# Attention and MLP gradients of one decode step: batch 1's middle paced differently, its kept heads moved in the second pass, and the MLP output in a stream of its own

## The chip, the cores and the metric

The kernel runs on one core of one Trainium2 chip. The metric is the device time of a launch in microseconds (us), the median of five runs. A profiled execution gives a span (first to last instruction) and a trace of every instruction and transfer.

## The reference

One decode step of a pre-norm transformer block, forward and backward: two sequences (B = 2), width D = 640, 32 heads of 128, a cache of 4096 keys and values for each head, an MLP of 1728 with ReLU.

```python
def _fwd_reference(A_x, A_k_cache, A_v_cache, A_wq, A_wo, B_x, B_w1, B_w2):
    ...
    h = x + _A_ref(_layernorm(x, axis=-1), A_k_cache, A_v_cache, A_wq, A_wo)
    h2 = h + _B_ref(_layernorm(h, axis=-1), B_w1, B_w2)
    return h2

def reference(A_x, A_k_cache, A_v_cache, A_wq, A_wo, B_w1, B_w2, B_x, grad_out):
    ...
    _out, _vjp = jax.vjp(_f, A_x, A_k_cache, A_v_cache, A_wq, A_wo, B_w1, B_w2)
    _grads = _vjp(grad_out)
```

`_A_ref` is softmax attention of one query against the cache, followed by `wo`. The eight outputs are the forward result (out_0) and the gradients of x (out_1), the K cache (out_2), the V cache (out_3), wq (out_4), wo (out_5), w1 (out_6) and w2 (out_7). The cache gradients are the bulk: 64 pairs of sequence and head, each with 1 MiB of K gradient and 1 MiB of V gradient in bf16.

## The kernel before

The work goes over the 64 pairs of batch and head twice.

*Pass one* (`p1_iter`, i = 0 to 65) loads K and V of a pair, transposes K on TensorE, computes scores, softmax, the attention output and a 128 x 128 matrix MT for each head. At its end for a batch, `middle_gen(b)` does what lies between forward and backward: output projection, layer norm, MLP forward, MLP backward, layer norm backward, and then, for groups of heads (`go_group`), the gradient of each head's output. The dot products with the rows of w1 (15 of them) and wo (32, one for each head) are VectorE instructions (L649, in `ttr`). `ln_fwd` and `ln_bwd` are chains of short VectorE instructions with small TensorE column sums between them.

*Pass two* (`p2_iter`, j = 0 to 64, called a turn here) takes one pair: it loads V again as W (L457, on SP's queue), transposes it as float32 pairs (L436), copies the result out of PSUM on ScalarE (L441), multiplies it with the head's output gradient (L449), forms the row of score gradients (gsp, L835), and makes the outer products gK and gV on VectorE (L822, two halves each). POOL's queue stores them (L860 and L879). The first turns run inside pass one; from i = 41 on every second iteration carries one, so that turns 0 to 12 lie there and turns 13 to 64 follow alone. `turns` gives the order: for each batch first the "kept" heads, whose V tile of pass one is kept in SBUF and not loaded again (six of batch 0, the last five, 27 to 31, of batch 1), then the others. Batch 1's kept heads stand at places 32 to 36.

Turn j of batch 1 needs its head's `go_group`. If that isn't done when the turn begins, `bg_until` runs the background to that mark at once.

The program is written out in one order for each engine by an interleaver. A turn has seven steps k = 0 to 6. After each step three background streams may go on: `bg` (the middle), `bg2` (`fin_gen`: the weight gradients out_7, out_6, out_5, out_4, as matmuls L926 into a PSUM bank and copies L935 and L933 into an "ot" tile, stored by ScalarE's queue) and `bg3` (`gx_gen`: the gradient of x through wq, as transposes L993, copies L995 and matmuls L1003). A stream earns credit at a rate in each step and spends it as its generator yields: 0.5 for a plain yield, or the number that it yields. `RATES` is for the middle, `RATE2` and `RATE3` for the others. `slot` says in which steps the middle may issue a dot product. `wait(n)` lets n x `spread` steps pass between a producer and its consumer.

`mlp_out` (out_0 = h + MLP forward) loads w2 in three parts and multiplies it (L709). Before, it is the end of batch 1's `middle_gen`, in stream `bg`.

The large tiles live in 12 "homes" of 1 MiB, and a thirteenth after w1's tile is released. Each belongs to a tag: `ld` (loads), `g` (gK, gV), `f` (output tiles), `q` (w2 and wq parts of the two streams). `share` sets how many each tag is to have; a home changes its tag when it is next given back. At turn 13 it is 8 for `ld` and 4 for `g`, of which the kept tiles hold 5; once the kept heads of batch 1 are through it is 4, 4, 3 and 2:

```python
        elif fin is not None and j >= H + KEPT[1] - 1:
            share(ld=4, g=4, f=3, q=2)
```

`fin_gen` and `gx_gen` begin at the turn after w1's dot products are done; `gx_gen` waits for every `go_group`.

Of the kernel before, what the change touches and what calls it, by code (L numbers as in the profile page):

```python
# [9 lines left out]
ALU = mybir.AluOpType  # L10
# [5 lines left out]
def kernel(  # L16
# [20 lines left out]
    nc = tc.nc  # L37

    B, Sq, D = A_x.shape
    _, H, Sk, Dh = A_k_cache.shape  # L40
# [17 lines left out]
    def f_kc(c):  # L58
        return 128 if c < NFF else F_rem
# [45 lines left out]
    def give(t, to=None):  # L105
        tag, k, _ = home_of.pop(id(t))
        to = to or goes_to(tag)
        owned[tag] -= 1
        owned[to] += 1
        free[to] += 1  # L110
        homes[to].append(k)
        given_at[k] = step[0]
# [25 lines left out]
    spread = [1]  # L138
# [253 lines left out]
    NP1 = len(pairs)  # L392
    KEPT = (6, 5)
    turns = [(b, h) for b in range(B) for h in (*range(H - KEPT[b], H), *range(H - KEPT[b]))]
    turn_of = {bh: j for j, bh in enumerate(turns)}
    kept = {(b, h) for b in range(B) for h in range(H - KEPT[b], H)}
    u_bank = [None]
# [254 lines left out]
    slot = [99]  # L652
# [42 lines left out]
    def mlp_out():  # L695

        ml32 = small.tile([128, ND, B], FP32, tag="ml32", bufs=1, name="ml32")
        nc.vector.memset(ml32[:], 0.0)
        for k in range(NW2):
            while free["q"] < 1:  # L700
                yield
            t = load_w2(k, "q", "(p c) d -> p c d")
            yield from wait(12)
            c1 = min(NF, (k + 1) * FP)
            m_ps = pst([128, ND, B], FP32, "mid", "mlp_ps")
            for c in range(ND):
                for cf in range(k * FP, c1):
                    kc = f_kc(cf)
                    nc.tensor.matmul(m_ps[:, c, :], lhsT=t[0:kc, cf - k * FP, c * 128:(c + 1) * 128],  # L709
                                     rhs=arow[0:kc, cf, :], start=(cf == k * FP), stop=(cf == c1 - 1))  # L710
            give(t)
            yield
            nc.vector.tensor_tensor(out=ml32[:], in0=m_ps[:], in1=ml32[:], op=ALU.add)
        ml_bf = small.tile([128, ND, B], BF16, tag="ml_bf", bufs=1, name="ml_bf")
        nc.vector.tensor_copy(out=ml_bf[:], in_=ml32[:])
        y_bf = small.tile([128, B, ND], BF16, tag="y_bf", bufs=1, name="y_bf")
        nc.vector.tensor_tensor(out=y_bf[:].rearrange("p b c -> p c b"), in0=h1c[:], in1=ml_bf[:], op=ALU.add)
        yield from wait(3)
        for b in range(B):
            store_row(y_bf[:, b, :], ND, out_0[b].rearrange("s (c p) -> (s c) p", p=128))  # L720
            yield

    def middle_gen(b):
        if o_next[0] < (b + 1) * H // OG:
            o_group()
        nc.vector.tensor_reduce(out=u4[:], in_=u_bank[0][:].rearrange("p (s d) -> p d s", s=4),
                                axis=AX.X, op=ALU.add)
        yield
        while a_next[0] < (b + 1) * H // OG:
            if a_next[0] == o_next[0]:  # L730
                o_group()
                yield
                yield
            a_group()
            yield
        at_bf = small.tile([128, ND], BF16, tag="at_bf", bufs=1, name="at_bf")
        nc.vector.tensor_copy(out=at_bf[:], in_=asum[:, b, :])
        nc.vector.tensor_tensor(out=h1c[:, :, b], in0=xg32[:, b, :], in1=at_bf[:], op=ALU.add)
        h32 = small.tile([128, 1, ND], FP32, tag="h32", bufs=1, name="h32")
        nc.vector.tensor_copy(out=h32[:, 0, :], in_=h1c[:, :, b])  # L740
        yield ("a", b)
        u_out(b)
        yield from ln_fwd(h32[:], 1, x2c[:, :, b:b + 1], rstd2[:, b:b + 1])
        hf_ps = pst([128, NF], FP32, "mid", "hf_ps")
        for cf in range(NF):
            kc = f_kc(cf)
            for c in range(ND):
                nc.tensor.matmul(hf_ps[0:kc, cf:cf + 1], lhsT=w1_t[:, c, cf * 128:cf * 128 + kc],
                                 rhs=x2c[:, c, b:b + 1], start=(c == 0), stop=(c == ND - 1))
            yield 0.25  # L750
        nc.vector.tensor_scalar(out=acol[:, 0:NFF, b], in0=hf_ps[:, 0:NFF], scalar1=0.0, scalar2=None, op0=ALU.max)
        if F_rem:
            nc.vector.tensor_scalar(out=acol[0:F_rem, NFF, b:b + 1], in0=hf_ps[0:F_rem, NFF:NF],
                                    scalar1=0.0, scalar2=None, op0=ALU.max)
        if b == B - 1:
            ar_ps = pst([128, NFF, B], FP32, "mid", "ar_ps")
            for cf in range(NFF):
                for c in range(ND):
                    nc.tensor.matmul(ar_ps[:, cf, :], lhsT=w1_t[:, c, bass.ds(cf, 128, step=NFF)],
                                     rhs=x2c[:, c, :], start=(c == 0), stop=(c == ND - 1))  # L760
                yield 0.25
            nc.vector.tensor_scalar(out=arow[:, 0:NFF, :], in0=ar_ps[:], scalar1=0.0, scalar2=None, op0=ALU.max)
            if F_rem:
                nc.vector.tensor_copy(out=arow[:, NFF, :], in_=acol[:, NFF, :])
        mask = small.tile([128, NF], FP32, tag="mask", bufs=1, name="mask")
        nc.vector.tensor_single_scalar(out=mask[:], in_=acol[:, :, b], scalar=0.0, op=ALU.is_gt)
        nc.vector.tensor_tensor(out=ghfc[:, :, b], in0=ga[:, b, :], in1=mask[:], op=ALU.mult)
        yield from wait(3)
        fbc = cols.tile([128, Dff], BF16, tag="fbc", name="fbc")
        gx2 = small.tile([128, 1, ND], FP32, tag="gx2", bufs=1, name="gx2")  # L770
        gx2p = small.tile([128, ND, 3], FP32, tag="gx2p", bufs=1, name="gx2p")
        FW = Dff // 3
        spread_f = bcast_cols(one(ghfc, b), NF, f_kc, fbc)
        have = 0
        for k in range(3):
            while have < min(Dff, (k + 1) * FW):
                next(spread_f)
                have += 512
                yield
            for c in range(ND):  # L780
                yield from turn()
                ttr(w1_t[:, c, k * FW:(k + 1) * FW], fbc[:, k * FW:(k + 1) * FW], gx2p[:, c, k:k + 1], FW)
                yield 0.85
        nc.vector.reduce_sum(out=gx2[:, 0, :], in_=gx2p[:], axis=AX.X)
        yield ("w1", b)
        yield from ln_bwd(gx2[:], x2c[:, :, b:b + 1], rstd2[:, b:b + 1], gc[:, :, b:b + 1], gh1c[:, :, b:b + 1], 1)
        hbc = cols.tile([128, D], BF16, tag="rowbc", name="hbc")
        yield from bcast_cols(one(gh1c, b), ND, lambda c: 128, hbc)
        yield ("gh1", b)

        first = H - KEPT[b]
        bounds = [(first, first + 2), (first + 2, H)] if b == 0 else [(first, H)]
        bounds += [(h, min(first, h + GH)) for h in range(0, first, GH)]
        for h0, h1 in bounds:
            yield from go_group(b, h0, h1, hbc)
        if b > 0:
            yield from mlp_out()

    def ga_gen():

# [221 lines left out]
    bg3 = []  # L1022
    done = set()
# [33 lines left out]
    M0_ITERS = 7  # L1057
    P2_AT = H + 2 + M0_ITERS
    RATES = (0.2, 0.8, 0.2, 0.8, 0.45)
    RATE2 = 0.65  # L1060
    RATE3 = 0.45
    plan = []
    i = j = 0
    while i <= NP1 + 1 or j <= NP1:
# [47 lines left out]
    fin = big2 = None  # L1112
# [12 lines left out]
    for n, (i, j) in enumerate(plan):  # L1125
# [4 lines left out]
            share(ld=KEPT[1] + 3, g=4)  # L1130
        if fin is not None and not bg2 and not bg3:
            share(ld=7, g=6)
        elif fin is not None and j >= H + KEPT[1] - 1:
            share(ld=4, g=4, f=3, q=2)
        if j is not None:
            while g2 is not None:
# [4 lines left out]
        if i is None and ("w1", 1) in done and fin is None:  # L1141
            wts.release()
            fin = tc.alloc_tile_pool(name="fin", bufs=1)
            big2 = tc.alloc_tile_pool(name="big2", bufs=1)
            more_home("f", big2)
            banks.update(sps=[2, 3], o=[4, 5, 6])
            bg2.append(("fin", fin_gen(fin)))
            bg3.append(("gx", gx_gen(fin)))
        late[0] = all(("go", B - 1, h) in done for h in range(H))
        if i == 12:  # L1150
# [7 lines left out]
        rate = RATES[0 if i is not None and i <= H + 1 else 1 if j is None and i < P2_AT else  # L1158
                     2 if i is not None else 3 if j <= H else 4]
        if i is None:  # L1160
            spread[0] = 2
            at_k[0] = 1
            k = 0
            while g2 is not None:
                p2_step()
                pump()
                slot[0] = int(k in ((1, 3, 5) if j <= H else (1, 4)))
                k += 1
                bg_step(0, rate)
                bg_step(1, RATE2)  # L1170
                bg_step(2, RATE3)
            continue
# [61 lines left out]
```

## Time and profile before

| | before |
|---|---|
| median of 5 runs | 940.1 us (937.7 to 940.52) |
| profiled execution | 939.73 us |
| its span | 938.0 us |
| moved by DMA | 363.02 MB, mean 387 GB/s |
| VectorE busy | 661.6 us, 71% |
| TensorE busy | 765.9 us, 82% |
| mean granted TensorE clock | 0.777 |
| stores of gK and gV | 64 each, 1024 KB, 10.5 and 11.2 us to landing |
| loads of W | 53, 1024 KB, 10.5 us to landing |

The page cuts the span into 40 slices of 23.4 us. Its digits are busy tenths; the row of GB/s is what the 16 DMA engines moved. An answer by windows gives for each stretch of time its length and the busy time of each engine, with the number of instructions in brackets, then the granted TensorE clock (1.00 is full), the mean busy share of the DMA engines, and GB/s. In the waits each line names who waited, for whom, the sum in us, how often, and the longest.

### The profile page before, as it was taken

The page shows a single profiled execution, that of the slowest core. Times are in us where ns is not written, and L with a number is a line of the kernel's source. Part 1 is how long each engine was busy: PE and PEld are TensorE (multiplying, and loading weights), DVE is VectorE, ACT ScalarE, POOL GpSimd, SP SyncE. Part 2 cuts the span into 40 slices and gives each one's busy share as a digit, 9 for nine tenths or more (in the row PEclk, how much of TensorE's full clock was granted, in tenths as well). Part 3 has the DMA queues.
Part 4 walks back from the last instruction along what each step waited for, and adds up shares of the span by engine and source line. Part 5 has one row for each costly group of instructions (what it writes and reads, how often), then busy time and mean ns, then how long its engine had stood idle before and what let it go on. Part 6 is the DMA issues. An engine that isn't in the chain of part 4 may idle for free.

```text
span 938.0 us, 26775 instructions
## 1 busy us (share of the span) xinstructions
PE 765.9 (82%) x11482; PEld 639.0 (68%) x11482; DVE 661.6 (71%) x1237; ACT 550.9 (59%) x1162; POOL 140.7 (15%) x249
## 2 busy tenths in 40 slices
PE   5999898999998888797977838686888887888882
PEld 5887687888787777686867726564666665675652
DVE  4655687766876888686777889887797555465675
ACT  4666566667776777675733626454665564566652
POOL 1222111121001101010012112111121011011111
PEclk9999999999997999899886856655555555565556
DMA  9999999997878999999999999999999999999998
GB/s 347 420 398 410 407 387 410 413 418 291 299 293 338 362 398 424 424 408 424 392 362 377 407 426 390 393 392 377 407 405 394 422 425 419 337 395 371 335 424 360
DMA packets 59478, 363.02 MB, mean 387 GB/s; under 512 B 5696, under 2 KB 15552, under 8 KB 19168
## 3 DMA queue, kind: packets, MB, share of 16 engines
q1 hardware_dynamic: 37920, 212.18, 57.8%
q0 software_dynamic: 18432, 134.23, 34.7%
q10 hardware_dynamic: 3008, 14.91, 4.1%
q8 instruction: 90, 1.47, 0.6%
q14 instruction: 28, 0.23, 0.1%
HBM read 212.16 MB, written 149.13 MB: 385 GB/s over the span
## 4 chain that ended last, share of the span: by engine, by line
PE 40%; DMA 25%; DVE 16%; ACT 11%; issue 6%; POOL 0%; POOLq 0%; SPq 0%; DVEq 0%; ACTq 0%
DMA Kt<-in_A_k_cache_dram 13%; PE t_ps L436 10%; DMA out_dram<-gK 9%; PE m_ps L470 7%; PE t_ps L415 6%; ACT t_sb L420 5%; DVE gV L822 5%; DMA out_dram<-gV 4%; DVE gK L822 4%; PE o_ps L926 4%; PE s_ps L426 3%; ACT t_sb L441 3%; DVE pk L477 2%; PE u_ps L495 2%; DVE junk L649 2%
## 5 line engine op out<-in xcount | busy, mean ns | idle before, releaser
L441 ACT COPY t_sb<-t_ps 128x512 f32<-128x512 f32 x256 | 149.8, 588 | 161.8 <-PE t_ps L436 158.9
L420 ACT COPY t_sb<-t_ps 128x1024 bf16<-128x1024 bf16 x223 | 216.6, 1012 | 46.1 <-PE t_ps L415 41.4
L436 PE MATMUL t_ps<-ident_f,Wt 128*128 128x128 f32 x848 | 193.8, 376 | 3.9 <-ACT t_sb L420 1.7
L470 PE MATMUL m_ps<-pk,Vt 128*128 128x129 bf16 x2048 | 191.6, 222 | 1.0 <-DVE pk L477 0.6
L477 DVE TENSOR_TENSOR pk<-Kt,ep 128x2048 bf16<-128x2048 bf16 x128 | 156.4, 1222 | 34.6 <-ACT ep L520 34.5
L822 DVE TENSOR_TENSOR gK<-rb,gsp 128x2048 bf16<-128x2048 bf16 x128 | 152.2, 1225 | 30.3 <-DMA out_dram<-gK 18.7
L822 DVE TENSOR_TENSOR gV<-rb,pp 128x2048 bf16<-128x2048 bf16 x128 | 152.8, 1219 | 24.2 <-DMA out_dram<-gV 19.9
L415 PE MATMUL t_ps<-ident_bf,Kt 128*128 128x128 bf16 x2048 | 153.4, 225 | 17.3 <-DMA Kt<-in_A_k_cache_dram 16.8
L436 PEld LDWEIGHTS t_ps<-ident_f,Wt 128*128 128x128 f32 x848 | 134.0, 194 | 35.7 <-issue 24.1
L470 PEld LDWEIGHTS <-Vt 128*128 128x128 bf16 x2048 | 128.6, 99 | 29.4 <-issue 29.4
L415 PEld LDWEIGHTS <-Kt 128*128 128x128 bf16 x2048 | 126.3, 101 | 20.0 <-DMA Kt<-in_A_k_cache_dram 19.4
L449 PEld LDWEIGHTS <-t_sb 128*128 128x128 bf16 x2048 | 96.8, 107 | 40.7 <-ACT t_sb L441 18.7
L426 PE MATMUL s_ps<-qc,t_sb 128*128 128x1 bf16 x2048 | 88.7, 164 | 19.0 <-ACT t_sb L420 17.7
L449 PE MATMUL dp_ps<-gom,t_sb 128*128 128x2 bf16 x2048 | 95.7, 168 | 9.0 <-ACT t_sb L441 8.0
L426 PEld LDWEIGHTS <-t_sb 128*128 128x128 bf16 x2048 | 75.1, 97 | 31.2 <-ACT t_sb L420 28.0
L879 POOL DMA_DIRECT2D out_dram<-gV x64 | 34.2, 534 | 288.4 <-DVE gV L822 231.5
L860 POOL DMA_DIRECT2D out_dram<-gK x64 | 34.0, 531 | 281.0 <-DVE gK L822 221.9
L566 POOL COPY P_bf<-ep 128x32 bf16<-128x32 bf16 x40 | 42.8, 1070 | 218.7 <-ACT ep L520 218.7
L935 ACT CAST ot<-o_ps 128x512 bf16<-128x512 f32 (+4 forms) x134 | 60.0, 478 | 20.5 <-DMA out_dram<-ot 11.7
L561 DVE TENSOR_REDUCE rmax<-s_ps 128x1 bf16<-128x32 f32 x64 | 12.3, 193 | 59.5 <-PE s_ps L426 59.5
L649 DVE CUSTOM_DVE_ANT_0 junk<-wo_t,hbc 128x640 bf16<-128x640 bf16 x64 | 52.4, 819 | 0.2
L582 ACT CAST MT<-m_ps 128x128 bf16<-128x128 f32 x64 | 17.1, 267 | 58.7 <-PE m_ps L470 58.7
(194 smaller groups left out, 821.9 us busy)
## 6 DMA issues: line engine op xcount, KB each, us to landing
Kt<-in_A_k_cache_dram SPq DMA_DIRECT2D x64, 1024.0 KB, 14.8
Vt<-in_A_v_cache_dram SPq DMA_DIRECT2D x64, 1024.0 KB, 11.3
out_dram<-gV POOLq DMA_DIRECT2D x64, 1024.0 KB, 11.2
out_dram<-gK POOLq DMA_DIRECT2D x64, 1024.0 KB, 10.5
Wt<-in_A_v_cache_dram SPq DMA_DIRECT2D x53, 1024.0 KB, 10.5
wo_t<-in_A_wo_dram SPq DMA_DIRECT2D x4, 1280.0 KB, 13.0
wqs<-in_A_wq_dram SPq DMA_DIRECT2D x5, 1024.0 KB
wq_t<-in_A_wq_dram SPq DMA_DIRECT2D x5, 960.0 KB, 15.0
```

Source lines behind the costliest of these rows:

```text
L415: nc.tensor.transpose(t_ps[:, j, :], nat[:, g * GT + j, :], ident_bf[:])
L420: nc.scalar.copy(out=t_sb[:], in_=t_ps[:])
L426: nc.tensor.matmul(dst[:, sc:sc + 1], lhsT=t_sb[:, j, :], rhs=vec, start=True, stop=True)
L436: nc.tensor.transpose(t_ps[:, j, :], natf[:, 2 * cc:2 * cc + 2, :].rearrange("p c k -> p (c k)"), ident_f[:])
L441: nc.scalar.copy(out=t_sb[:], in_=t_ps[:])
L449: nc.tensor.matmul(dst[:, sc:sc + 2], lhsT=v[:, j, :, par], rhs=vecs[:, par, :], start=(par == 0), stop=(par == 1))
L470: nc.tensor.matmul(r["m"][:, 0:129], lhsT=r["V"][:, sc, :], rhs=r["pk"][sc // HALF][:, sc % HALF, 0:129], start=(sc == 0), stop=(sc == NSC ...
L477: nc.vector.tensor_tensor(out=p["pk"][k][:, :, 0:128].rearrange("p s (a two) -> p s a two", two=2), in0=p["K"][:, sl, :].rearrange("p s (a ...
L566: (nc.gpsimd if i < P2_AT else nc.vector).tensor_copy(out=P_bf[:, bhp, :], in_=ep[:, :, 0])
L649: nc.vector.tensor_tensor_reduce(out=junk[0:kc, 0:width], in0=in0, in1=in1, scale=1.0, scalar=0.0, op0=ALU.mult, op1=ALU.add, accum_out=acc)
L822: nc.vector.tensor_tensor(out=pairs_view(dst[:, sl, :]), in0=row.rearrange("p (a two) -> p a two", two=2)[:, None, :, :].to_broadcast([128 ...
L935: nc.scalar.copy(out=ot[0:P, k, n0:n0 + nn], in_=o_ps[0:P, 0:nn])
```

## The change

The kept heads of batch 1 are taken at places 22 to 26 of the second pass, ahead of the last ten heads of batch 0, and the homes are shared out anew from turn 26 instead of 36. Until the kept group of batch 1 is done, a turn may issue a dot product of the middle in five of its seven steps (0, 1, 3, 4, 5) instead of three; afterwards in two. Until w1's dot products are done, `wait` counts single steps. `mlp_out` leaves the middle and becomes the first entry of `bg3`, ahead of `gx_gen`; its addition comes directly behind the matmuls, before the yield. `RATE2` goes from 0.65 to 0.58, `RATE3` from 0.45 to 0.35.

```diff
     turns = [(b, h) for b in range(B) for h in (*range(H - KEPT[b], H), *range(H - KEPT[b]))]
+    KEPT1_AT = 22
+    turns[KEPT1_AT:H + KEPT[1]] = turns[H:H + KEPT[1]] + turns[KEPT1_AT:H]
...
             give(t)
+            nc.vector.tensor_tensor(out=ml32[:], in0=m_ps[:], in1=ml32[:], op=ALU.add)
             yield
-            nc.vector.tensor_tensor(out=ml32[:], in0=m_ps[:], in1=ml32[:], op=ALU.add)
...
             yield from go_group(b, h0, h1, hbc)
-        if b > 0:
-            yield from mlp_out()
...
-    RATE2 = 0.65
-    RATE3 = 0.45
+    RATE2 = 0.58
+    RATE3 = 0.35
...
-        elif fin is not None and j >= H + KEPT[1] - 1:
+        elif fin is not None and j >= KEPT1_AT + KEPT[1] - 1:
             share(ld=4, g=4, f=3, q=2)
...
             bg2.append(("fin", fin_gen(fin)))
+            bg3.append(("mlp", mlp_out()))
             bg3.append(("gx", gx_gen(fin)))
...
         if i is None:
-            spread[0] = 2
+            spread[0] = 2 if ("w1", B - 1) in done else 1
+            hurry = ("go", *turns[KEPT1_AT]) not in done
...
-                slot[0] = int(k in ((1, 3, 5) if j <= H else (1, 4)))
+                slot[0] = int(k in ((0, 1, 3, 4, 5) if hurry else (1, 4)))
```

## The prediction

> **What bounds the kernel now.** I read the page's 40 slices first, then the stage windows, cut where the POOL timeline shows the gV store of a turn being issued, then the waits.
>
> ```profile
> span 938.0 us, 26775 instructions
> ...
> PEclk9999999999997999899886856655555555565556
> DMA  9999999997878999999999999999999999999998
> GB/s 347 420 398 410 407 387 410 413 418 291 299 293 338 362 398 424 424 408 424 392 362 377 407 426 390 393 392 377 407 405 394 422 425 419 337 395 371 335 424 360
> ```
>
> The DMA engines are busy nearly throughout. Holes: slices 10 to 14 (batch 0's middle, in pass one, which the diff doesn't touch), and 35 and 38. The change starts at 481 us, so that stretch counts:
>
> ```profile
> core 0: us, PE busy (x) PEld busy (x) DVE busy (x) ACT busy (x) POOL busy (x), PEclk, DMA share, GB/s
> 481.83:556.62 74.79, 49.59 (x677) 43.26 (x675) 57.93 (x104) 30.22 (x56) 12.22 (x27) 0.71 1.00 405
> 556.62:633.40 76.78, 56.37 (x550) 45.87 (x551) 68.73 (x123) 38.34 (x85) 14.48 (x30) 0.59 1.00 394
> 633.40:679.91 46.51, 35.55 (x310) 27.73 (x308) 33.52 (x58) 25.02 (x58) 6.52 (x15) 0.50 0.99 393
> 679.91:743.18 63.27, 52.87 (x466) 40.51 (x463) 48.37 (x77) 35.99 (x77) 12.12 (x25) 0.50 1.00 406
> 743.18:806.61 63.43, 51.76 (x523) 39.37 (x523) 34.47 (x41) 34.30 (x71) 7.83 (x18) 0.55 0.99 408
> 806.61:887.24 80.63, 67.30 (x643) 51.92 (x642) 46.55 (x64) 48.41 (x95) 10.93 (x24) 0.54 0.96 360
> 887.24:926.74 39.50, 30.27 (x288) 20.93 (x286) 28.33 (x35) 21.41 (x40) 7.33 (x15) 0.63 1.01 424
> 926.74:937.95 11.21, 0.00 (x0) 0.00 (x0) 2.30 (x2) 0.00 (x0) 1.06 (x2) 0.50 0.69 289
> ```
>
> The rows are turns 13-21, 22-31, 32-36 (kept heads of batch 1), 37-44, 45-50, 51-58, 59-63, and the drain. The last column against 424 GB/s, the best stage, gives what each loses: length x (1 - rate/424) = 3.4, 5.4, 3.4, 2.7, 2.4, 12.2, 0 and 3.6 us, 33 us together. That is all that any reordering here can win. In turns 22-31 VectorE is 90% busy; in 51-58 it isn't (58%), and TensorE stands at 83%. The waits of 780 to 900 us say what holds the late stores:
>
> ```profile
> POOL out_dram L860 <- DVE gK L822: 47.2, 10, 7.2
> POOL out_dram L879 <- DVE gV L822: 42.0, 11, 6.4
> ACT t_sb L441 <- PE t_ps L436: 28.0, 36, 2.5
> DVE ot L933 <- PE o_ps L926: 18.1, 8, 4.0
> DVE gsp L835 <- PE dp_ps L449: 15.0, 8, 4.7
> PE o_ps L926 <- ACT ot L935: 13.4, 14, 1.6
> ```
>
> Stores wait for VectorE, VectorE for TensorE (ot, gsp), TensorE for ScalarE's ot copies. So the hole in turns 51-58 is TensorE and ScalarE serving three streams at a half clock. It comes in bursts: turns 50, 51, 55 and 56 took 14.0, 16.7, 11.7 and 14.9 us from gV store to gV store, turns 52, 57 and 58 6.5, 8.2 and 5.6.
>
> **What the Trainium skill says.** "DMA: Bandwidth & Descriptors", section "Where 436 GB/s comes from", gives a fabric ceiling of 435 GB/s; the trace's best stages are at 424, so they are full. "Perfetto Trace Analysis", section "Identifying the Most-Contended Engine", warns that occupancy of 16 DMA engines misleads and bytes per time should be used; the trace agrees (626-633 us: share 1.01, 331 GB/s). "VectorE: DVE Perf Modes", section "The perf-mode tier table (the rule you actually need)", puts a bf16 tensor_tensor of 2048 elements at 1224 ns, capped at 2x; the trace has 1219 and 1225, so a turn's four gK/gV halves can't get cheaper.
>
> **The change, part by part.** A turn is a p2_iter of seven background steps k = 0..6. I counted yields, credits and homes for both orders; for before, the count gives w1 done in turn 22, the kept group in 26, first wqs load in 41, all background done in 60, and the trace has those in 22, 26, 40-41 and 59-60.
>
> Pass one is the same, so nothing before 481 us moves.
>
> (1) *Hurry.* Five dot products (L649) a turn instead of three, and waits of one step each instead of two until w1 is done. By count w1 ends in turn 18, the kept group in turn 21 at k=6, the last step before turn 22 demands it; so bg_until forces nothing, or a few steps if I am one off. Price on VectorE: a turn's own work is 4 x 1.22 + 0.28 (gsp) = 5.16 us. A w1 dot product takes 0.79 us from start to start in the timeline, a wo one 0.87. Turns 16, 17, 18: 5.16 + 5 x 0.79 = 9.1 us; turn 20: 9.5; turn 19 (ln_bwd, memset): about 7.5. A turn writes 2 and reads 1 MiB, 3.15 MB, 7.4 us at 424 GB/s. VectorE is over by 3 x 1.7 + 2.1 = 7.2 us. Cover: transfers already issued. A store lands 10.5 to 11.2 us after issue, so some 4 MB or 9 us stand in the queues, and DMA drains them before it idles. Uncovered, all 7.2 us. I take **+3** (0 to +7).
>
> (2) *Less VectorE later.* Turns 22-31 issue 16 dot products instead of 20, without ln_bwd and kept group: some 6 us less of 68.7. DMA sets most of the pace there: **-1** (-3 to 0).
>
> (3) *Kept heads at 22-26.* No instruction more or less: the same 53 W loads, the same stores. Freed homes are refilled with W up to eight ahead, as at 32-36. The third home for outputs and two for q come at turns 26-29 instead of 36-39. With one f home ScalarE waited twice for an ot store (11.7 us in two waits of about 6), and everything in order behind it on ScalarE, t_sb first. The wait for the second tile stays, that for the third goes: **-1** (-3 to 0), as DMA was running beside it.
>
> (4) *MLP stream.* Its five w2 loads on SP go from turns 41-48 to 28-35, before W loads that are four or more turns ahead: nothing. Its 150 matmuls (3.2 us) leave the burst. Its add now follows the matmuls with no step between, so VectorE, with the next gV half behind it and POOL's store behind that, waits for TensorE; before, two such waits made 7.8 us. Three of 2 to 4 us, mostly covered by queued transfers: **+0.5** (0 to +3). The rows of out_0 (1.2 KB) move past wqs loads on SP for nothing.
>
> (5) *Rates.* Output and q streams get 0.93 credits a step instead of 1.10. By count: output matmuls of out_5 begin in turn 38 instead of 42, all ends in 59 instead of 60, gx runs in 42-56 instead of 43-59, since mlp no longer takes a q home from it. Prices from 721-906 us: base 108.3 us of TensorE in 18 turns (L436, L449, L844), an output matmul 0.43, a gx group of eight (L993, L1003) 1.29; lines overlap, since they add up to 185 and the engine shows 154, so times 0.83: 5.0, 0.36, 1.07. A burst turn now has 8 matmuls and 3 groups: 5.0 + 2.9 + 3.2 = 11.1 us, and as TensorE never fills over 0.83 of a stage, 13.4; turns 50 and 55 show 14.0 and 11.7. Afterwards the common turn of 42-54 has 7 and 1 or 2: 9.1 us, or 11.0 at 0.83. Its DMA: 3.15 + 7 x 0.082 + 1.5 x 0.26 = 4.1 MB, 9.7 us. Without the fill limit nothing is lost: -12. With it, 12 turns x 1.3 = 16 us over, less 9 queued, 7 lost against 14.6 (turns 45-58): -7.6. I take **-7** (-12 to +3).
>
> Sum: 3 - 1 - 1 + 0.5 - 7 = -5.5. The profiled execution took 939.7 us (938.0 span and 1.7 around it), 0.4 below the median of the five. 939.7 - 5.5 = **934**.
>
> **The rivals.**
>
> *The hurry stalls engines in order (slower).* All 7.2 us of (1) are uncovered, and with half the distance between hand-overs the layer norm's short steps block: with two steps between, the chain of turns 13-16 already showed waits of 5.3 (a_ps), 4.4 and 3.6 us (ar_ps). Two us more at each of four makes 8. That is 15, less 7 won late: 948. It decides once the early loss passes 9 us. For: VectorE is at 77% in turns 13-21 and gets 10 us more in 75. Against: in 507-557 it was at 77% (38.55 of 49.8) and DMA still moved 417 GB/s.
>
> *TensorE's plateau.* The streams no longer pause for each other, so twelve turns in a row are TensorE's at 11 us or more; the late gain is gone or turned: 940 to 944. For: 0.50 to 0.55 clock. Against: turn 47 alone reaches 7 and 3.
>
> *The holes only move.* Bytes are the same and DMA is busy; early loss equals late gain: 939 to 941.
>
> **Numbers.** Forecast (late hole shrinks) 0.64, of which nearly all is faster; hurry stalls 0.16; plateau 0.12; holes move 0.08. About 0.2%, 2 us, is what a measurement of this kernel can tell. Faster 0.66, same 0.10, slower 0.24. All the good ends give 922, all the bad ones over 950; range 924 to 945.
>
> **What would show it.** Right: the kept group's L690 around turn 21, no wait over 3 us before turn 22's L835; turns 16-20 at 8 to 9.5 us with DMA at 390 or more; one long ACT wait on an ot store; turns 45-58 without any above 12 us and at 390 GB/s or more. Wrong: GB/s under 370 in turns 16-21 (hurry), or turns 42-54 at 11 us with TensorE at 83% (plateau), or L684 pushed out by forced steps at turn 22.

## The result: slower by a third of a per cent, and the profile after

The changed kernel takes 942.72 us in the median of 43 runs, against 940.53 us for the kernel before (80 runs). The ratio is 1.0034 with a 95% interval of 1.0022 to 1.0046: slower, by some 3 us (the two medians stand 2.2 us apart). The forecast was 934, a gain. The profiled execution took 944.07 us.

From the page of the changed kernel, the slices:

```profile
span 942.2 us, 26764 instructions
...
PEclk9999999999999999897985755565555755765556
DMA  8999999997878999999997999999999999999998
GB/s 348 419 399 409 408 393 410 412 417 267 300 290 332 364 354 423 424 422 411 411 387 288 406 355 393 407 385 409 416 406 400 425 387 389 379 414 344 415 425 367
```

The low slices 35 and 38 of before are higher now (379 and 415), but two new ones stand at 22 (288) and 24 (355). Those are turns 13 to 15 and turns 19 to 21. Slices 33, 34 and 37 have fallen too (387, 389 and 344, from 425, 419 and 371). The windows, cut by the same turns as in the prediction (13-21, 22-31, 32-36, 37-44, 45-50, 51-58, 59-63, drain):

```profile
core 0: us, PE busy (x) PEld busy (x) DVE busy (x) ACT busy (x) POOL busy (x), PEclk, DMA share, GB/s
483.28:563.92 80.64, 52.07 (x648) 46.33 (x645) 66.19 (x138) 30.84 (x62) 12.52 (x27) 0.62 0.92 359
563.92:641.09 77.17, 63.88 (x575) 50.00 (x575) 64.13 (x105) 42.60 (x96) 15.12 (x30) 0.59 1.00 397
641.09:687.77 46.68, 36.83 (x356) 27.35 (x356) 32.53 (x55) 25.25 (x55) 7.01 (x16) 0.50 1.01 413
687.77:762.79 75.02, 57.07 (x555) 43.26 (x556) 47.18 (x72) 40.34 (x88) 10.44 (x24) 0.61 1.01 411
762.79:821.62 58.83, 49.70 (x501) 38.34 (x501) 33.34 (x38) 34.65 (x68) 7.83 (x18) 0.57 0.98 377
821.62:894.62 73.00, 59.71 (x561) 42.23 (x558) 47.12 (x63) 44.13 (x85) 11.41 (x25) 0.61 0.98 392
894.62:931.12 36.50, 24.06 (x262) 19.76 (x259) 25.58 (x28) 16.09 (x30) 8.20 (x16) 0.64 1.01 424
931.12:942.15 11.03, 0.00 (x0) 0.00 (x0) 2.29 (x2) 0.00 (x0) 1.06 (x2) 0.50 0.73 305
```

Read the last column first: 405 has become 359 in the first row, 408 has become 377 in turns 45-50, and 360 has become 392 in turns 51-58. Both kernels move the same 363.02 MB, so a ledger of lost transfer time explains the span. Its entry for a stage is length x (1 - rate/424), summed over finer stages (13-15, 16-21, 22-26 and so on):

| us lost against 424 GB/s | before | after | difference |
|---|---|---|---|
| turns 13-15 | 2.6 | 6.6 | +4.0 |
| turns 16-21 | 0.8 | 5.7 | +4.9 |
| turns 22-26 | 1.8 | 1.9 | +0.1 |
| turns 27-41 | 9.8 | 6.6 | -3.2 |
| turns 42-58 | 14.6 | 11.9 | -2.7 |
| turns 59-63, drain | 3.6 | 3.1 | -0.5 |

The sum is +2.6. Another 1.5 us of the 4.2 between the spans lies ahead of turn 13, where the two programs are the same: that stretch took 479.5 to 486.6 us in the 19 profiles of this study. The early loss is 9 us, the late gain 6. The late gain is itself a balance: turns 51-58 lose 6.7 us less than before, turns 42-50 lose 4.0 us more.

Two windows of the changed kernel split the early part (turns 13-15, 16-21):

```profile
483.28:515.40 32.12, 22.44 (x319) 20.99 (x317) 19.88 (x50) 9.12 (x17) 3.92 (x10) 0.59 0.86 337
515.40:563.92 48.52, 29.63 (x331) 25.34 (x330) 46.31 (x89) 21.72 (x46) 8.60 (x18) 0.64 0.96 374
```

The third group of busy columns is VectorE. In turns 13-15 it is 62% busy and the three turns still take 7 us more than before (25.0). In turns 16-21 it is busy 95% of the time: the first suspect there. For turns 13-15 the VectorE waits, of before and then of after (who waited, for whom, us, times, longest; one wait of 0.2 us in each is left out):

```profile
DVE gK L822 <- DMA out_dram<-gV: 4.0, 1, 4.0
DVE gV L822 <- DMA out_dram<-gK: 0.7, 1, 0.7
```

```profile
DVE gK L822 <- DMA out_dram<-gV: 4.5, 1, 4.5
DVE arow L764 <- PE ar_ps L761: 3.9, 1, 3.9
DVE ln_mean L238 <- PE csum L222: 1.6, 1, 1.6
DVE gsp L835 <- PE dp_ps L451: 1.3, 2, 1.1
```

Three waits on TensorE, 6.8 us together, have appeared, about the extra time of the stage. The timeline of VectorE shows what stands behind the longest:

```profile
505.98 2.36 DVE L822 TENSOR_TENSOR gK<-rb,gsp 128x2048 bf16<-128x2048 bf16 x2
512.26 0.18 DVE L764 TENSOR_SCALAR arow<-ar_ps 128x26 bf16<-128x26 f32 x1 [3.93 <-PE ar_ps L761]
...
512.74 2.36 DVE L822 TENSOR_TENSOR gV<-rb,pp 128x2048 bf16<-128x2048 bf16 x2
```

Turn 15's gV stands in order behind arow. Before, a wait of 3.6 us for the same result came two turns later; single steps bring the hand-over forward, and turn 13's column sum (1.6 us) is not ready either.

The longer time is not where most transfer time is lost, though. Turn by turn, most of it goes in two turns, 14 (4.6 of the 6.6 us) and 19 (2.7 of the 5.7). Before, these moved 357 and 421 GB/s; now:

```profile
497.24:504.74 7.50, 4.71 (x106) 4.25 (x105) 6.96 (x19) 1.94 (x4) 1.31 (x3) 0.73 0.52 164
540.24:547.80 7.56, 5.17 (x46) 4.63 (x47) 7.05 (x18) 2.46 (x5) 1.30 (x3) 0.50 0.77 272
```

From 501 to 503 us DMA moves nothing. That is ahead of the wait for arow (508.3 to 512.3), during which turn 15 moves 387 GB/s. What comes late for turn 14 is the work of turns 13 and 14 on VectorE:

```profile
494.58 2.36 DVE L822 TENSOR_TENSOR gV<-rb,pp 128x2048 bf16<-128x2048 bf16 x2
...
498.00 1.23 DVE L822 TENSOR_TENSOR gK<-rb,gsp 128x2048 bf16<-128x2048 bf16 x1
...
500.96 1.22 DVE L822 TENSOR_TENSOR gK<-rb,gsp 128x2048 bf16<-128x2048 bf16 x1
```

The layer norm's wait of 1.6 us and its short steps stand ahead of turn 13's gV and between the halves of turn 14's gK. These stores go out 14.0 and 19.2 us after turn 13 begins; before, it was 11.6 and 15.1. In turns 17 and 18 VectorE is busy without a gap (8.34 of 8.41 us, 8.33 of 8.40) and DMA still moves 397 and 423 GB/s; it runs dry in turn 19.

### The profile page after: what moved, and what is told of

Read it like the earlier page. It is cut to its first block, busy times and chain, and to the rows that moved or that the text cites. A ratio compares the mean times of both kernels' runs of the same rounds, so it can differ in the third digit from the quotient of the medians.

```text
span 942.2 us, 26764 instructions
## 1 busy us (share of the span) xinstructions
PE 768.4 (82%) x11482; PEld 639.7 (68%) x11482; DVE 660.4 (70%) x1234; ACT 551.2 (58%) x1165; POOL 142.0 (15%) x249
## 2 busy tenths in 40 slices
DMA packets 59478, 363.02 MB, mean 385 GB/s; under 512 B 5696, under 2 KB 15552, under 8 KB 19168
## 4 chain that ended last, share of the span: by engine, by line
PE 36%; DMA 30%; DVE 19%; ACT 8%; issue 5%; POOL 0%; SPq 0%; POOLq 0%; ACTq 0%; DVEq 0%
DMA out_dram<-gV 14%; DMA Kt<-in_A_k_cache_dram 10%; PE m_ps L472 8%; PE t_ps L438 7%; PE t_ps L417 6%; DVE gV L822 6%; DMA out_dram<-gK 6%; ACT t_sb L422 5%; PE s_ps L428 4%; DVE gK L822 4%; DVE junk L651 3%; DVE pk L479 3%; PE o_ps L926 3%; PE u_ps L497 2%; PE dp_ps L451 1%
## 5 line engine op out<-in xcount | busy, mean ns | idle before, releaser
L438 PE MATMUL t_ps<-ident_f,Wt 128*128 128x128 f32 x848 | 196.2, 379 | 3.2 <-ACT t_sb L995 1.8
L417 PE MATMUL t_ps<-ident_bf,Kt 128*128 128x128 bf16 x2048 | 155.3, 227 | 15.9 <-DMA Kt<-in_A_k_cache_dram 15.9
L417 PEld LDWEIGHTS <-Kt 128*128 128x128 bf16 x2048 | 128.0, 102 | 18.1 <-DMA Kt<-in_A_k_cache_dram 17.8
L428 PE MATMUL s_ps<-qc,t_sb 128*128 128x1 bf16 x2048 | 89.0, 164 | 19.1 <-ACT t_sb L422 17.6
L849 ACT ACTIVATE rb<-dp_ps,rt 128x256 bf16<-128x256 f32 x64 | 30.6, 478 | 44.8 <-PE dp_ps L844 43.4
## 6 DMA issues: line engine op xcount, KB each, us to landing
Kt<-in_A_k_cache_dram SPq DMA_DIRECT2D x64, 1024.0 KB, 14.1
out_dram<-gV POOLq DMA_DIRECT2D x64, 1024.0 KB, 11.2
Wt<-in_A_v_cache_dram SPq DMA_DIRECT2D x53, 1024.0 KB, 10.5
wo_t<-in_A_wo_dram SPq DMA_DIRECT2D x4, 1280.0 KB, 15.7
wqs<-in_A_wq_dram SPq DMA_DIRECT2D x5, 1024.0 KB, 11.1
```

The costliest lines, as they stand in the source:

```text
L417: nc.tensor.transpose(t_ps[:, j, :], nat[:, g * GT + j, :], ident_bf[:])
L428: nc.tensor.matmul(dst[:, sc:sc + 1], lhsT=t_sb[:, j, :], rhs=vec, start=True, stop=True)
L438: nc.tensor.transpose(t_ps[:, j, :], natf[:, 2 * cc:2 * cc + 2, :].rearrange("p c k -> p (c k)"), ident_f[:])
```

## The experiments

Each is timed against runs of the kernel before beside it. The chip is not the same for all, so compare ratios rather than medians. "Early" and "late" are the ledger's sums for turns 13-26 and from 27 on, in us, each from one profiled execution and worked out over the stretch as a whole (which can differ by 0.3 us from a sum of stages). A profile can stand up to 5 us from its kernel's median, so ratios decide, and the ledger says where. How far an entry repeats can be read from the table: the six kernels without hurry and single steps (before, r_only, p27_only, p27_m, p27_mr, w_5835) lose 5.2 to 6.9 us early, the four with both at full length (changed, w_hs, a_6038c, a_oldrates) 14.1 to 16.6.

| kernel | ratio (95% interval) | early | late |
|---|---|---|---|
| before | 1 | 5.2 | 27.7 |
| changed | 1.0034 (1.0022 to 1.0046) | 14.1 | 21.6 |
| single steps alone (s_only) | 1.0074 (1.0050 to 1.0099) | 12.6 | 22.6 |
| single steps in the layer norm (s_ln) | 1.0002 (0.9981 to 1.0023) | 10.2 | 21.7 |
| hurry alone (h_only) | 1.0055 (1.0035 to 1.0074) | 13.1 | 24.2 |
| the same, short products (h_short) | 0.9983 (0.9963 to 1.0002) | 6.9 | 20.8 |
| changed, short products (a_short) | 1.0005 (0.9982 to 1.0029) | 11.4 | 20.7 |
| rates alone (r_only) | 0.9991 (0.9972 to 1.0009) | 6.8 | 22.5 |
| place 27 alone (p27_only) | 1.0028 (1.0011 to 1.0045) | 5.5 | 31.3 |
| place 27 and MLP stream (p27_m) | 1.0023 (1.0004 to 1.0042) | 6.3 | 29.5 |
| the same, rates 0.60, 0.38 (p27_mr) | **0.9932 (0.9907 to 0.9957)** | 6.9 | 16.6 |
| that with hurry, single steps (w_hs) | 1.0107 (1.0071 to 1.0144) | 15.1 | 22.4 |
| p27_mr at 0.58, 0.35 (w_5835) | 1.0056 (1.0035 to 1.0077) | 6.8 | 25.1 |
| changed, place 24, two steps (a_at24_spr2) | 0.9993 (0.9972 to 1.0015) | 11.2 | 19.9 |
| changed, two steps (a_spr2c) | 1.0027 (1.0010 to 1.0043) | 16.8 | 19.1 |
| changed, 0.60 and 0.38 (a_6038c) | 1.0003 (0.9983 to 1.0022) | 15.2 | 18.1 |
| changed, old rates (a_oldrates) | 1.0137 (1.0095 to 1.0180) | 16.6 | 30.2 |

**Single steps alone.**

```diff
-            spread[0] = 2
+            spread[0] = 2 if ("w1", B - 1) in done else 1
```

> The kernel before with one edit: waits of the middle count single steps until w1 is done (spread 1). Theory A (the short steps of the layer norm and of the MLP forward, issued closer together, stall VectorE and TensorE in order in turns 13-15, where the trace of the changed kernel is 7 us longer than before): slower by 3 to 7 us, turns 13-15 at 29 us or more against 25.0, DMA there below 360 GB/s. Theory B (the five dot products a turn make VectorE the bound in turns 16-20): no difference, within 2 us. Theory C (the kept heads' new place or the later streams cost it): no difference.

947.14 us. Turns 13-15 took 31.5 us at 351 GB/s, close to the changed kernel's 32.1 and 337: A is right on these turns and on the total, B and C on their own are not. But these turns lose only 2.8 us more than before, and turns 16-21 lose 3.9 more, of which A said nothing.

**Hurry alone.**

```diff
+            hurry = ("go", *turns[H]) not in done
...
-                slot[0] = int(k in ((1, 3, 5) if j <= H else (1, 4)))
+                slot[0] = int(k in ((0, 1, 3, 4, 5) if hurry else (1, 3, 5) if j <= H else (1, 4)))
```

> The kernel before with one edit: five steps of a turn may issue a dot product until the kept group of batch 1 is done, three as before afterwards; waits as before. Theory A: within 2 us of before. Theory B: slower by 3 to 7 us, with turns 18-22 at 9 us or more and DMA below 390 GB/s in them. Theory C: no difference.

944.25 us. Turn 17 took 12.2 us, turns 18-20 8.4 each (B had said 9 or more), at 379 GB/s over turns 16-21. B is right too on the total and the rate: each of the two edits costs by itself. Turns 13-15 lose 2.4 us here, as before; turns 16-21 then lose 5.4 and turns 22-26 another 5.4.

**The hurry with short dot products.**

```diff
-                ttr(w1_t[:, c, k * FW:(k + 1) * FW], fbc[:, k * FW:(k + 1) * FW], gx2p[:, c, k:k + 1], FW)
+                wd = 64 if b == B - 1 else FW
+                ttr(w1_t[:, c, k * FW:k * FW + wd], fbc[:, k * FW:k * FW + wd], gx2p[:, c, k:k + 1], wd)
```

> The kernel with the hurry alone, its fifteen w1 dot products of batch 1 cut to 64 of 576 columns each (the rest of those products is left out): the same instructions in the same places with some 0.6 us less of VectorE each. Theory B (VectorE's time is what the hurry costs in turns 16-21, where the hurry alone loses 5.4 us of transfer time against 0.8 before): that loss falls to 2 us or less, the time to 939-942 us. Rival (the position of the instructions, or the earlier output stream behind them, costs it): stays at 943 to 945.

937.83 us, below the 939 to 942 expected; from 1.0055 to 0.9983. The windows of turns 16-21, first with whole products, then with short ones:

```profile
504.76:555.77 51.01, 31.91 (x374) 29.02 (x373) 41.98 (x75) 18.40 (x35) 8.79 (x18) 0.58 0.97 379
```

```profile
506.26:552.63 46.37, 33.14 (x391) 30.13 (x391) 34.28 (x77) 19.51 (x39) 9.56 (x18) 0.61 1.01 406
```

With 7.7 us of VectorE work gone, 4.6 us of the stage go and DMA is back at 406. The stages behind it lose less too (22-26: 2.3 against 5.4). What the hurry costs here is mostly VectorE's time. The kernel before with the same short products was not run, so what the cut is worth without the hurry is open; turns 16-21 lose only 0.8 us there.

**The changed kernel with short dot products** (the same diff).

> The changed kernel with the fifteen w1 dot products of batch 1 cut to 64 of 576 columns (the rest of them left out): some 9 us less VectorE time in turns 16-18, all else in place. Theory B (VectorE is the bound of the hurried turns): faster than the changed kernel by 4 to 9 us, 934 to 939 us, loss of turns 16-21 at 3 us or less against 5.7. Rival (the order of the instructions costs, not VectorE's time): within 2 us of the changed kernel.

940.16 us, a ratio of 1.0005 against 1.0034, about 2.7 us less: short of the 4 to 9 expected, and the two intervals overlap. Turns 16-21 lose 3.1 instead of 5.7, as expected; turns 13-15 lose 6.5 as before. So VectorE's load is part of the early loss in the changed kernel, and what turns 13-15 lose is another part that it doesn't touch.

**Which single step?** s_ln sets single steps until batch 1's layer norm is through, and two afterwards.

> The kernel before with single-step waits inside batch 1's layer norm only, two steps afterwards. Theory A1 (what single steps cost is the layer norm's chain, which now stands ahead of turn 13's gV and is met by TensorE results that aren't ready: waits of 1.6 and 1.3 us on VectorE and 2.1 on TensorE that the kernel before doesn't have): as slow as the kernel with single steps up to w1, 945 to 948 us, turns 13-15 at 29 us or more. Rival A2 (the later chain, the MLP forward and its broadcast, costs it): within 2 us of before.

938.9 us, no slower than before, although turns 13-15 took 32.2 us. The hole of turn 14 is there too (213 GB/s), and A1 still falls as a statement on the total. The windows of turns 16-21, with single steps up to w1, then in the layer norm alone:

```profile
514.84:561.92 47.08, 26.74 (x304) 23.54 (x303) 41.64 (x70) 18.09 (x35) 8.60 (x18) 0.61 0.95 382
```

```profile
513.35:560.67 47.32, 27.01 (x320) 23.20 (x319) 40.44 (x65) 19.12 (x35) 8.32 (x18) 0.64 1.01 410
```

The turns are as long, but DMA catches up in the second: early loss 10.2 against 12.6. That is 2.4 us of the 7 between the ratios, and little more than early entries differ by anyway. The rest is not explained. By its ratio s_ln is no slower than before although it loses 5 us more early: its profile loses 6 us less late. An edit to the early turns also shifts which instructions of the output and gx streams fall into which later turn; call that the late order.

**The wait for the MLP forward.** Both kernels leave out the 65 matmuls behind arow; the first has single steps, the second doesn't.

```diff
-                for c in range(ND):
-                    nc.tensor.matmul(ar_ps[:, cf, :], lhsT=w1_t[:, c, bass.ds(cf, 128, step=NFF)],
-                                     rhs=x2c[:, c, :], start=(c == 0), stop=(c == ND - 1))
                 yield 0.25
-            nc.vector.tensor_scalar(out=arow[:, 0:NFF, :], in0=ar_ps[:], scalar1=0.0, scalar2=None, op0=ALU.max)
+            nc.vector.memset(arow[:, 0:NFF, :], 0.0)
```

> The kernel with single steps up to w1, without the 65 matmuls that compute the MLP forward in its second layout (that part of out_0 is left out). Theory A1: VectorE's wait of 3.9 us in turn 15 is gone with about 4 us of turn 15, but the layer norm's waits stay: still slower than the next kernel by 3 us or more. Theory A3 (that one wait, standing ahead of gV in turn 15 where nothing is queued any more, is the whole cost): no more than 1 us slower than the next kernel.

> The kernel before without the same 65 matmuls (that part of out_0 is left out), for comparison. Its VectorE wait of 3.6 us in turn 16 goes. All theories: same as before or faster by up to 3 us, as turns 16-21 lose only 0.8 us of transfer time there.

942.26 us (ratio 1.0039, 1.0011 to 1.0068) and 938.83 us (0.9992, 0.9975 to 1.0009). Turns 13-15 fell from 31.5 to 26.5 us, but turns 16-21 rose from 47.1 to 51.3, and early losses stayed at 12.8. A3 falls and A1 holds here: with the longest wait gone the single steps still cost 0.5%.

**The late part, edit by edit.** Rates alone:

> The kernel before with one edit: rates 0.58 and 0.35. Theory D (the lower rates keep the output and q streams from piling up on TensorE and ScalarE in one turn, whatever else is done): faster by 3 to 8 us, the loss of turns 51-58 under 6 us against 12.2. Rival E (they help only where the streams begin earlier; here they end in turns 61 and 64 and hang over the end): same or slower by up to 5 us, with fewer turns of 5 to 7 us at the end.

939.46 us: E, not D, in the total, though turns 51-58 lost 7.9 instead of 12.2.

Place 27 alone (`KEPT1_AT = 27`), then with the MLP stream:

> The kernel before with one edit: the kept heads of batch 1 at places 27 to 31 and the homes shared out from turn 31, no hurry, old waits, old rates. Theory D: the output stream gets its three homes five turns earlier and stops being held up by them, so that at the old rates it piles up: same or slower by up to 4 us, loss of turns 37-50 above 6 us against 5.2. Rival F (earlier homes are a gain by themselves, from less waiting on ot stores): faster by 2 to 5 us.

> The kernel before with the kept heads at places 27 to 31 and the MLP output in a stream of its own ahead of gx, old waits, hurry and rates. By count gx then begins in turn 47 instead of 43 and ends in 59. Theory D: within 2 us of the kernel with the place alone, as the MLP has only some 3 us of TensorE. Rival G (the MLP stream puts the gx stream's work into fewer turns and so costs): slower than the place alone by 3 us or more.

942.01 and 942.69 us: earlier homes at the old rates cost 0.3% (D), though the new loss lies more in turns 27-36 (11.1 us against 7.0) than where D looked, in 37-50 (6.3 against 5.2). The MLP stream costs nothing that shows.

The changed kernel at the old rates:

> The changed kernel with the old rates of the two later streams (0.65 and 0.45). Theories A and B (the loss is early; the lower rates help late): slower than the changed kernel by 1 to 4 us, 944 to 947, with bursts of turns above 12 us in 40-56 and an earlier end of the streams. Theory C in the form that the lower rates cost: faster than the changed kernel, 940 or less.

953.56 us: 1% worse than with the new rates, more than twice the most expected. The late loss is 30.2 against 21.6. The lower rates are worth little alone and 10 us in the changed kernel.

**Without hurry and single steps.** Place 27, MLP stream, rates 0.60 and 0.38:

> The kernel before with the kept heads at places 27 to 31, the MLP stream of its own, and rates 0.60 and 0.38: the changed kernel's late part without its hurry and its single steps. Theory H (the early loss of about 9 us is the hurry's and the single steps', the late part is a gain of 2 to 6): 935 to 939 us, faster than before. Rival: within 1 us of before or slower, as place 27 and the MLP stream cost 2 us by themselves at the old rates and the lower rates alone gained under 1.

931.77 us, faster than both kernels. Hurry and single steps put back in:

> The kernel with the kept heads at places 27 to 31, the MLP stream and rates 0.60 and 0.38, and now the hurry and the single-step waits put back. Theory H (hurry and single steps lose some 9 us of transfer time in turns 13-26 and that isn't made up): slower than without them by 5 to 10 us, 937 to 942 us; turns 13-26 lose 12 to 15 us against 6.8. Rival I (the early loss is given back later, and what costs is the place 22): within 2 us of it, 930 to 934 us.

949.3 us, 1.8% more by the ratios, beyond the 5 to 10 us expected. Early losses went from 6.9 to 15.1, just the 8 to 9 us of the changed kernel; the other 6 us of the ledger are late ones.

> The same kernel without hurry and single steps, at the changed kernel's own rates 0.58 and 0.35, so that it differs from the changed kernel only in hurry, single steps and place. Theory H: 930 to 937 us, 5 us or more below the changed kernel. Rival (0.60 and 0.38 are what makes the fast kernel fast): 939 us or more, as by count the output stream ends only in turn 64.

944.16 us: Theory H failed here. Place, stream and early part are as in the fastest kernel, and it is slower than before; nor is it faster than the changed kernel (1.0034), though it loses 7 us less early. Turns 51-58 of the two, p27_mr first:

```profile
799.02:876.72 77.70, 70.42 (x681) 51.36 (x680) 44.83 (x53) 49.45 (x95) 10.45 (x25) 0.57 0.99 406
```

```profile
799.64:886.82 87.18, 65.56 (x681) 50.28 (x678) 44.61 (x49) 48.36 (x93) 10.47 (x24) 0.60 0.92 364
```

The same 681 matmuls take 9.5 us longer; two turns of 17.1 and 14.4 us, against 9.7 and 9.6, hold all of it. The waits in the first of them:

```profile
DVE gsp L835 <- PE dp_ps L451: 9.6, 1, 9.6
```

VectorE stands for TensorE's last product of a turn, as in the bursts of the kernel before. So rates of 0.65 and 0.45, 0.60 and 0.38, 0.58 and 0.35 give ratios of 1.0023, 0.9932 and 1.0056: where output and gx streams meet seems to decide, not the rate as such. No run places that meeting directly, so this stays a reading of the traces. That bursts come from the order and not from chance is shown by the two kernels before with and without the 65 matmuls: turns 50, 51 and 56 took 14.0, 16.7 and 14.9 us in both.

**Two steps in the changed kernel.** First with place 24, where nothing is forced, then at place 22:

> The changed kernel with waits of two steps throughout, and the kept heads at places 24 to 28 so that their group (by count done in turn 23 at step 6) needs no forced steps. Theory A: the early loss goes and the late gain stays: 3 to 7 us less than the changed kernel, so 936 to 940 us, faster than before by 0 to 4. Theory B: as slow as the changed kernel, 942 to 944. Theory C: as slow as the changed kernel.

> The changed kernel with waits of two steps throughout; by count the kept group is eight steps short when turn 22 demands it, and bg_until issues them at once. If single steps are what costs in the changed kernel: turns 13-15 back at 25 us, the loss of turns 13-26 at 9 to 12 us with the forced steps in turn 22, the total 938 to 941 us. If the forced steps cost as much as the single steps did: 942 to 945, with turns 22 and 23 together above 20 us.

939.13 and 941.98 us. Turns 13-15 are back at 25 us in both. At place 24 the total is the one that A expected, but the early loss only falls to 11.2, as the hurry is still there. At place 22 turn 22 then takes 15.7 us: the forced steps stop TensorE for 4.9 us (pr_ps for goc), turns 22-26 lose 8.6, and the early loss is 16.8, not the 9 to 12 expected. By the ratios single steps and forced steps cost about the same; place 22 needs one of them.

**The changed kernel at 0.60 and 0.38.**

> The changed kernel at rates 0.60 and 0.38, those of the fastest kernel so far. Theory H (hurry and single steps lose 9 us early, and what the late part gains depends finely on how the rates make the output stream meet the gx stream): the early loss of turns 13-26 stays at 13 to 15 us whatever the total, which comes out anywhere from 937 to 950 us, as the late part moves. Rival J (0.60 and 0.38 are simply better rates): 934 to 938 us.

940.34 us: neither rate pair makes the changed kernel faster than before; the early loss is 15.2, about the 13 to 15 that H says. J falls. Set beside w_hs (1.0107), which has hurry, single steps and the same rates at place 27, it is 1% faster: it is not the place 22 that costs, and rival I falls. (The two also differ in the slots of the few turns after the hurry, two steps against three.)

## Why the prediction was wrong

- **Step (1), the hurry, was mis-sized: +3 taken, +9 measured.** The load on VectorE was about right: turns 16-18 took 8.0 to 8.4 us (9.1 forecast), turn 20 9.6, and the kept group's last instruction came at 564.3 us, where turn 21 ends, without forced steps. Turns 16-21 lost 4.9 us more than before, within the 0 to 7.2. The other 4.0 us, in turns 13-15, were not in the sum: halving the waits was priced at nothing there and stood only in the rival.
- **The cover was taken as twice what stood there.** The 10.5 to 11.2 us from issue to landing were read as a queue of 9 us. But a store needs time even with little ahead of it: the one issued at 496.9 us in the kernel before, as DMA fell to 115 GB/s, landed after 5.8 us. Those of its turns 15 and 16, where the overload was to begin, took 9.7 to 10.3. The difference, some 4 us, is an estimate of what was queued. In the changed kernel stores took 8.5 to 11.4 us in turns 15-17 and 7.5 and 7.7 in turn 18; then turn 19 ran dry. The waits of turns 13-15 did not use the cover up: the hurry alone keeps these turns as before and loses 5.4 us in turns 16-21 all the same.
- Steps (2) and (3), VectorE relief and earlier homes: -2 taken, turns 27-41 gained 3.2. ScalarE's waits for ot stores fell from 11.7 to 2.0 us. The runs do not part the two.
- Step (4), MLP stream: +0.5 taken; VectorE waited 0.3 us for it, and no cost shows.
- **Step (5), the rates: -7 taken, -2.7 measured** in turns 42-58. The old rates would have cost the changed kernel 10 us, but with the kept heads at place 27 and no hurry the lower ones are the slower (1.0056 against 1.0023), so what failed is more than a size. Bursts stayed: turn 53 took 15.8 us, with gsp waiting 6.7 us for TensorE. A mean of 11 us for a turn does not describe them. The limit that TensorE fills no more than 0.83 of a stage is not one either: in p27_mr it is busy for 0.91 of turns 51-58. (The base of TensorE work adds up to 112.4 us in the trace, not 108.3; scaled to the engine's busy time it stays 5.0 us a turn.)
- The rival "hurry stalls engines in order" named both early losses, and put the limit at an early loss of 9 us. It came to 9.0, and the late gain of 6 was smaller than it. Its price (15 early) was too high: it counted two us more at each wait, and VectorE's wait for ar_ps only went from 3.6 to 3.9 us and cost nothing early that shows.
- The rival "plateau" came true in part: turns 45 to 49 took 9.6 to 11.8 us each, TensorE was 84% busy in 45-50, and that stage went from 408 to 377 GB/s. This took 4 us off the gain of turns 51-58.

## What to carry to other kernels

A transfer's time to landing is not the depth of the queue ahead of it: before pricing an overload as covered, take off what a transfer needs with little ahead of it (here 5.8 us of some 10). Then read each wait beside the rate of transfers, turn by turn. The longest wait here, 3.9 us, stood in a turn that moved 387 GB/s, and taking it out left the early loss as it was; the hole at zero stood behind a chain of short steps, ahead of long instructions on the same engine. And a stream's rate in a hand-made order is not a dial: three near settings gave 0.7% faster, 0.2% and 0.6% slower, so a gain worked out from average load per turn needs the turns where streams meet.

## What the runs showed that I had not expected

Taking 65 matmuls out of the order left early losses as they were (12.6 and 12.8 us) and only moved them from turns 13-15 to 16-21. At the old rates the edits nearly add: single steps, hurry, and place with MLP stream sum to 1.5% (with place 27; 1.4% measured together, at place 22). The rates don't: worth 0.1% alone, they took 1% off that. And an early loss need not reach the total: s_ln lost 10.2 us early against 5.2 and was no slower than before.
